# A planned order and engine choice replaced from its 346th operation on

## The chip, the cores and the metric

The kernel runs on one core of a Trainium2 chip. The metric is the device time of one execution in microseconds (us), lower being better. The engines are named as the profile names them: PE (matrix multiply; PEld is its loading of the stationary operand), DVE, ACT and POOL (element-wise work), SP (which issues nearly all DMAs).

## What is computed

Attention with a local window and block summaries, and then two layers that each expand 512 channels to 2048, apply an element-wise function and come back to 512. Cut to what matters:

```
# attention: 2 x 8 heads, 768 positions, 64 channels
k_sum = k.reshape(B, H, 24, 32, D).max(axis=3)
v_sum = v.reshape(B, H, 24, 32, D).mean(axis=3)
scores = concat(local scores within 16 positions, q @ k_sum + log 32)
x = softmax(scores) @ concat(v, v_sum)            # 1536 rows of 512
# first layer
h = x @ w_in                                      # 512 -> 2048
g = (a0 + a1 h + a2 h^2 + a3 h^3) / (1 + |b0 h| + |b1| h^2)
x = g @ w_out                                     # 2048 -> 512
# second layer
h = x @ w_in2
out = (h * cos(h)) @ w_out2
```

## The kernel before

Every matrix product of the two layers is made of three products of a high and a low part (`gh`, `gl` for the activations, two halves of `w` for the weights), which the function `split` makes: one copy to a rounded type (L347 on ACT, L349 on POOL, L352 on DVE) and one subtraction (L806 on POOL or DVE). The weights come from memory as 64-bit numbers into one of three `raw` buffers and are turned to 32 bits by three DVE steps (L789, L793, L797).

The 1536 rows are handled in three blocks of 512. For each block and each slice of 128 of the 2048 inner channels there is a unit: the products into `h` (L946), the element-wise chain (`ew1`, `ew1s` in the first layer: L1233 to L1259; `ew2` in the second: L1314 and L1317 reduce the angle, L1320 is the Sin on ACT, L1323 the product), a `split` into `gh` and `gl`, and four times three matmuls into four accumulators `acc` (L1363, in `mlp_o`). Most units are handled two or four at a time with seven products in place of eight, whose sums share PSUM banks: `mlp_h4` (L1133, 512 columns) and `mlp_h2` (L1182, 256 columns). There a bank that goes on accumulating has first to be read out by a copy (`keep`, on ACT or DVE) or an addition (`plus`, L1146 on DVE), so a later product waits for that read. When PE turns from one block to the next, the four accumulators are spilled to `part` or `room` (L341, L343, L347, L352 by engine) and the sums of the next block are copied back into the same four banks (L347 or L352, out `acc`); the first triple of matmuls into a bank waits for its copy. The attention is interleaved with the first units: transposes of k and q (`ktp`, `qtp`), scores (`sp`, L652), the softmax (L682 on DVE, L686 on ACT, L703 the multiply by the reciprocal sum on POOL or DVE), its transpose (`ptp`, L716) and the product with v (`avp`, L763).

None of this is issued in the order in which the code stands. Each operation is recorded in a `Plan` with the engines that it may run on, and the string `ORDER` gives for each of the 3011 recorded operations which one comes next and which engine takes it:

```
for lo, hi, e in zip(raw[:n], raw[n:2 * n], raw[2 * n:]):
    o = rest.pop(lo + 256 * hi)
    o.eng = "AVPTS"[e]
```

Each engine then executes its own operations in exactly that order. `place` gives every tile the buffer that has been free longest in the same order, so buffers follow from the order too. Nothing in the program holds a time; semaphores between the engines keep the dependences.

Of the kernel before, what the change touches and what calls it, by code (L numbers as in the profile page):

```python
# [35 lines left out]
for _p, _t in (("AA", .143), ("AP", .17), ("AT", .25), ("AV", .14), ("PA", .08), ("PP", .08), ("PT", .15),  # L36
# [25 lines left out]
    "&L_k4w+`9agD1q)+$@PD=GjGSP0hX|m9g7y&DvP;(i8I}gVgE18@+Kj=e}3mQ#Z@O5l$TMBil~HfUv+kx_EHi#q9iXcCt6kf"
    "n75`=|QBa@Au(~dfctQw!d$FXW#+P{J+Wl>X4P-{ik@%82qJI{eIigo0!r|!Kaj_u?XYH`hr?s#_1c&60e02*2i}5IMn0@<b"
    "tq}L}W#-7T#hH<b3LEhGDt<F#H?5qcDLMej%FJ{CVVsq3L<1CI0t2{}Twa+X?vZ>l<KKk2R}aGx!g_&VQW`oIwIz+n)Uh`oF"
    "4=+GW??+^p*;V&Xgx9<vW{dv)EHuYKRYIE(7)=BK~+lU11K?}jMq(x^?6@UFS~e$0c=^V6jB{kp88IL~wcadGDDH(#Cvn;^c"
    "K#NMj$7v408{EaVXtIW?5Kknmw=Up7Uhs*mg4D&ddhtdAj3--acx+of=elq!_@w~wEi^-($KkNT2t8+iia<3?})JsdxGr*~X"
    "*z@xI0^ocYoU~1X*oq<x(obhWavs=`1H=?$QE)qZnPoPKI}tI%V2ruUj#g>PB0>x@C$b={GCx>^0PJ4@&@`L_5O4rm%c<RF2"
    "R3Ye^P5b>NA?j!(J}<!uDfi(A+)q8d_{<?=8FWTQ<-Fthi+Qt4OQZKp|nb>!=a4M&YX~#CV3#+V0|Hob$PKovKGYLnA6>s(9"
    "M3g=ojSGimc{K()L3?tlPdP4QZO=p+5e>w%d!zTe9WFzaPD=VKJ?%Sw56y3(KqXN%qfmUgei`v&q&p%U~ZLA16sZ&*DBy+xa"
    "#n%^SLk!^LtER{3>UWEUZAgQSwhnFNp?r{U)2I`l8V56->m%%AQ$Ag<#P?+4&WKUsJ9-laRCVAs~RG9uITq(H3FsV(Bkjkpt"  # L70
    "D5L}kx;DX~Nr*Lw9bb5Mh!!8c3SHFBkht-2Qh2``ZIx!5B))xEo*6JTbzb{wo$`q?*4jC{wjuX1-e+*%GU(KVizRJVN<g?<u"
# [1533 lines left out]
```

## Time and profile before

| | us |
|---|---|
| median of 3 runs | 590.38 (589.5 to 591.62) |
| the profiled execution | 591.18 |
| its span, first to last instruction | 589.4 |
| PE busy | 573.8 (97% of the span) |
| DVE busy | 529.1 (90%) |
| ACT busy | 451.3 (77%) |
| POOL busy | 355.7 (60%) |

The granted clock of PE is 1.00 over the span. A matmul is on record for longer than the step to the next one, since matmuls overlap, so a PE that is busy on the page may still lose time: how fast it goes is read from the distance of one matmul's start to the next. In the chain of work that ended last, 73% of the span is PE's, and ACT and DVE have 10% each.

### The profile page before, as it was taken

Reading aid. Unit: us, or ns where it says so; the run is one execution under the profiler, and the core shown is the slowest. Engines: PE = TensorE matmul, PEld = TensorE weight load, DVE = VectorE, ACT = ScalarE, POOL = GpSimd, SP = SyncE. Lnnn points to the kernel's source line nnn. Section 1 sums busy time; section 2 is a strip of 40 time slices with the busy share of each in tenths; the row PEclk is TensorE's granted clock in tenths of the full one; section 3 lists DMA queues with packets and bytes.
Section 4 is the critical chain, followed back from the end, with each engine's and each line's share of the span. In section 5 each row is a group of like instructions: output and inputs, shape, how many; then the busy total and the mean of one; then the engine's idle time right before and its main releaser. Section 6 shows DMA issues by size and latency. Waiting matters only on the chain.

```text
span 589.4 us, 10346 instructions
## 1 busy us (share of the span) xinstructions
PE 573.8 (97%) x3564; PEld 476.9 (81%) x3564; DVE 529.1 (90%) x1070; ACT 451.3 (77%) x979; POOL 355.7 (60%) x354
## 2 busy tenths in 40 slices
PE   8879999999999999999999999999999999999997
PEld 7568788888887887888888788888889888888885
DVE  4999999999999999999999999998889897886673
ACT  4989999989889999999899996757447335545343
POOL 4678889765878767777877625347354532554430
PEclk9999999999999999999999999999999999999999
DMA  8988950312122121312103221222231132020004
GB/s 254 245 225 224 252 131 16 112 31 65 51 71 71 41 103 37 108 48 97 53 20 107 73 72 37 71 72 72 72 107 49 62 106 72 1 72 1 1 37 178
DMA packets 68861, 51.83 MB, mean 88 GB/s; under 512 B 37304, under 2 KB 63160, under 8 KB 68808
## 3 DMA queue, kind: packets, MB, share of 16 engines
q1 hardware_dynamic: 68664, 51.03, 29.1%
q8 instruction: 28, 0.46, 0.3%
q14 instruction: 25, 0.20, 0.1%
q10 hardware_dynamic: 144, 0.13, 0.1%
HBM read 47.71 MB, written 3.15 MB: 86 GB/s over the span
## 4 chain that ended last, share of the span: by engine, by line
PE 73%; ACT 10%; DVE 10%; DMA 2%; issue 2%; SPq 1%; POOL 1%; ACTq 0%; DVEq 0%; POOLq 0%
PE acc L1363 34%; PE h L1133 15%; PE h L946 12%; PE h L1182 6%; PE avp L763 2%; ACT sc L686 1%; PE ptp L716 1%; PE sp L652 1%; DVE tt L1246 1%; DVE h L1256 1%; DVE tt L1253 1%; DVE h L1244 1%; DVE tt L1259 1%; DMA raw<-in_moe_w_out_dram 1%; DMA part<-in_k_dram 1%
## 5 line engine op out<-in xcount | busy, mean ns | idle before, releaser
L1363 PE MATMUL acc<-gh,w 128*128 128x512 f32 (+1 forms) x416 | 122.7, 378 | 1.3 <-ACT acc L347 1.3
L1363 PE MATMUL acc<-w,gh 128*128 128x512 f32 x382 | 118.1, 390 | 0.1
L806 POOL TENSOR_TENSOR gl<-tt,gh 128x512 fp32r<-128x512 f32 (+1 forms) x58 | 77.2, 1333 | 58.4 <-DVE gh L352 31.3
L1363 PEld LDWEIGHTS acc<-gh,w 128*128 128x128 f32 x416 | 75.4, 188 | 16.7 <-ACT acc L347 2.4
L1363 PEld LDWEIGHTS acc<-w,gh 128*128 128x128 f32 x382 | 70.5, 188 | 14.2 <-ACT part L341 0.6
L1363 PE MATMUL acc<-gl,w 128*128 128x512 f32 (+1 forms) x208 | 77.6, 373 | 0.0
L1363 PE MATMUL acc<-w,gl 128*128 128x512 f32 x191 | 74.3, 389 | 0.0
L806 POOL TENSOR_TENSOR w<-f,w 128x512 fp32r<-128x512 f32 x47 | 64.4, 1376 | 14.2 <-ACT w L347 13.0
L347 ACT COPY tt<-h 128x512 f32<-128x512 f32 (+1 forms) x68 | 35.2, 528 | 23.6 <-PE h L1133 10.5
L946 PE MATMUL h<-big,w 128*128 128x512 f32 x216 | 52.9, 390 | 0.2 <-DVE tt L1259 0.2
L1320 ACT ACTIVATE h<-h 128x512 f32<-128x512 f32 x48 | 27.3, 582 | 27.2 <-DVE h L1317 27.2
L946 PEld LDWEIGHTS h<-big,w 128*128 128x128 f32 x216 | 40.4, 188 | 9.1 <-DVE tt L1259 0.8
L797 DVE SCALAR_TENSOR_TENSOR f<-raw,f 128x512 int32<-128x512 int32 x64 | 47.4, 743 | 0.3
L1314 ACT ACTIVATE h<-tt 128x512 int32<-128x512 f32 x48 | 28.4, 601 | 24.9 <-DVE tt L1146 7.6
L793 DVE SCALAR_TENSOR_TENSOR f<-raw,f 128x512 int32<-128x512 int32 x64 | 44.7, 701 | 0.2
L1363 PEld LDWEIGHTS acc<-gl,w 128*128 128x128 f32 x208 | 39.1, 188 | 7.1
L1363 PEld LDWEIGHTS acc<-w,gl 128*128 128x128 f32 x191 | 35.8, 188 | 7.5
L1133 PE MATMUL h<-xH,w 128*128 128x512 f32 x120 | 41.5, 389 | 0.0
L347 ACT CAST gh<-tt 128x512 fp32r<-128x512 f32 (+1 forms) x56 | 34.6, 618 | 8.0 <-DVE tt L1323 4.5
L1323 DVE TENSOR_TENSOR tt<-tt,h 128x512 f32<-128x512 f32 x48 | 32.1, 681 | 7.2 <-ACT h L1320 6.9
L1242 POOL TENSOR_TENSOR tt<-tt,tf 128x512 f32<-128x512 f32 x21 | 29.1, 1386 | 14.1 <-ACT tt L1233 13.8
L686 ACT ACTIVATE sc<-sc,mn 128x120 f32<-128x120 f32 x96 | 37.5, 397 | 0.1
(261 smaller groups left out, 1572.1 us busy)
## 6 DMA issues: line engine op xcount, KB each, us to landing
raw<-in_moe_w_in_dram SPq DMA_DIRECT2D x32, 512.0 KB, 3.8
raw<-in_moe_w_out_dram SPq DMA_DIRECT2D x32, 512.0 KB, 3.3
vw<-in_v_dram SPq DMA_DIRECT2D x24, 192.0 KB, 4.1
qk<-in_q_dram SPq DMA_DIRECT2D x10, 256.0 KB, 3.7
out_dram<-part SPq DMA_DIRECT2D x8, 256.0 KB, 2.3
part<-in_k_dram SPq DMA_DIRECT2D x8, 192.0 KB, 3.7
big<-in_v_dram SPq DMA_DIRECT2D x3, 512.0 KB, 8.0
qk<-in_k_dram SPq DMA_DIRECT2D x6, 256.0 KB, 4.5
```

The lines of the kernel that those rows point to most:

```text
L347: nc.scalar.copy(out=o, in_=i)
L686: lambda e, pr=pr, hh=hh, sv=sv: nc.scalar.activation(out=sv()[:, pr, :], in_=sv()[:, pr, :], func=ACTF.Exp, scale=-1.0, bias=mn.t[:, hh, ...
L793: lambda e: nc.vector.scalar_tensor_tensor(out=ft.t.bitcast(I32), in0=lohi()[1], scalar=-0x40000000, in1=ft.t.bitcast(I32), op0=ALU.bitwis ...
L797: lambda e: nc.vector.scalar_tensor_tensor(out=ft.t.bitcast(I32), in0=lohi()[0], scalar=29, in1=ft.t.bitcast(I32), op0=ALU.logical_shift_r ...
L806: lambda e: E[e].tensor_tensor(out=lo(), in0=x(), in1=hi().bitcast(F32), op=ALU.subtract),
L946: nc.tensor.matmul(out=h.t[:, 0:n], lhsT=lt, rhs=rt[:, kk, cs], start=(k0 == 0 and i == 0), stop=(k0 == 2 and i == 5))
L1133: nc.tensor.matmul(out=bank.t, lhsT=lt, rhs=rt, start=start and i == 0, stop=stop and i == 5, skip_group_check=True)
L1182: nc.tensor.matmul(out=bank.t[:, c], lhsT=lt, rhs=rt, start=start and i == 0, stop=stop and i == 5, skip_group_check=True)
L1242: lambda e: E[e].tensor_tensor(out=U(), in0=U(), in1=Z(), op=ALU.add))
L1314: lambda e: nc.scalar.activation(out=H().bitcast(I32), in_=S_(), func=ACTF.Identity, scale=1.0 / PER, bias=0.25))
L1323: lambda e: E[e].tensor_tensor(out=S_(), in0=S_(), in1=H(), op=ALU.mult))
L1363: nc.tensor.matmul(out=dst, lhsT=lt, rhs=rt, start=(un.start and not have and i == 0), stop=(un.stop and i == 2), skip_group_check=have)
```

## The change

The string `ORDER` is another one. Nothing else in the program differs: the same 3011 operations with the same operands, of which 971 run on DVE in place of 974, 876 on ACT in place of 877, 327 on POOL in place of 323, and 696 on PE and 141 on SP as before. The order and the engines were searched anew, on a replay that was given the landing times of the DMAs as a trace showed them and the load of ACT's function table. The first 345 operations are the same, which in the trace of before reach to about 51 us on each engine.

```diff
 ORDER = (
-    "c-rk)$&Mt+aW&s!-}faWBDcz=GHc1&y0-3SZ!^Qeh>M0C5`>81ff(^XP#|?7bf6$m2VF=VBuJky2LbvFopcd&67(~4H;*E}K"
...
+    "c-rk*NslE-QZ`>A!eig#MZ}AUx9>}?l}oK%dv*6P>QT)wNQkOFphnX)!w7^pa6rQ#1V}9oAS8al`~WUo;K;AyfV+8Q&4~*qg"
...
 )
```

Three places in the order are shown here. The first is ACT at the turn from the first layer to the second, where the table for Sin is loaded; `acc_4262`, `acc_4267` and `acc_4266`, `acc_4289` are accumulators into which the next block's sums are copied back, the other `acc` are the finished ones that are spilled. Before:

```order
L341 ACTIVATE part<-acc_4116 128x512
L1251 ACTIVATE h<-tf 128x512
L341 ACTIVATE part<-acc_4172 128x512
L347 COPY acc_4262<-part 128x512
L347 COPY acc_4267<-part 128x512
L1320 ACT_TABLE_LOAD
L1320 ACTIVATE h<-h 128x512
L341 ACTIVATE part<-acc_4140 128x512
L341 ACTIVATE part<-acc_4089 128x512
L347 CAST gh<-tt 128x512
L347 COPY acc_4308<-part 128x512
```

The same place in ACT's order after the change:

```order
L1251 ACTIVATE h<-tf 128x512
L341 ACTIVATE part<-acc_4069 128x512
L347 COPY acc_4266<-part 128x512
L1320 ACT_TABLE_LOAD
L1320 ACTIVATE h<-h 128x512
L341 ACTIVATE part<-acc_4189 128x512
L341 ACTIVATE part<-acc_4145 128x512
L347 COPY acc_4289<-part 128x512
L347 CAST gh<-tt 128x512
L341 ACTIVATE part<-acc_4139 128x512
L347 COPY acc_4301<-part 128x512
```

One accumulator in place of two is spilled and refilled ahead of the load, and the third copy into an accumulator no longer stands behind a `gh` cast; PE's two small groups (L1182) stand behind one triple into a refilled accumulator, where they stood behind two.

The second place is PE within one `mlp_h4` of the first layer, at 185.8 us of the trace of before; `xL,pt`, `qT,pt` and so on are the operands of its products. Before:

```order
L1133 MATMUL h<-xL_111,pt 128x512
L1133 MATMUL h<-xH_110,qk 128x512
L1133 MATMUL h<-qT_2030,pt 128x512
L1133 MATMUL h<-qT_2032,pt 128x512
L1133 MATMUL h<-qT_2030,qk 128x512
L1133 MATMUL h<-sc,pt 128x512
L1133 MATMUL h<-pt 128x512
L1133 MATMUL h<-sc,qk 128x512
L1363 MATMUL acc_2748<-gh,w_2236 128x512 x2
L1363 MATMUL acc_2748<-gl,w_2236 128x512
L1363 MATMUL acc_2775<-gh,w_2236 128x512 x2
L1363 MATMUL acc_2775<-gl,w_2236 128x512
```

The same products in PE's order after the change:

```order
L1133 MATMUL h<-xL_111,pt 128x512
L1133 MATMUL h<-xH_110,qk 128x512
L1363 MATMUL acc_2684<-gh,w_2228 128x512 x2
L1363 MATMUL acc_2684<-gl,w_2228 128x512
L1363 MATMUL acc_2684<-gh,w_2359 128x512 x2
L1363 MATMUL acc_2684<-gl,w_2359 128x512
L1133 MATMUL h<-qT_2018,pt 128x512
L1133 MATMUL h<-qT_2043,pt 128x512
L1133 MATMUL h<-qT_2018,qk 128x512
L1133 MATMUL h<-sc,pt 128x512
L1133 MATMUL h<-pt 128x512
L1133 MATMUL h<-sc,qk 128x512
```

Two triples into an accumulator now stand between two products that stood back to back, and three triples follow ahead of the next product (`qk,w`) where two did.

The third place is DVE in the stage of the attention, some 200 rows into its list. Before, around a reciprocal (L699) of the softmax:

```order
L352 COPY room<-big 128x8x96
L806 TENSOR_TENSOR gl<-tt,gh 128x256
L699 RECIPROCAL su<-su 128x8
L352 CAST xH_110<-avp 128x4x128
L774 TENSOR_TENSOR xL_111<-avp,xH_110 128x4x128
L797 SCALAR_TENSOR_TENSOR f<-raw,f 128x512
```

And in the changed order:

```order
L789 TENSOR_SCALAR f<-raw 128x512
L774 TENSOR_TENSOR xL_111<-avp,xH_110 128x4x128
L699 RECIPROCAL su<-su 128x8
L703 TENSOR_TENSOR sc<-sc,su 128x480 x2
L793 SCALAR_TENSOR_TENSOR f<-raw,f 128x512 x2
L797 SCALAR_TENSOR_TENSOR f<-raw,f 128x512 x2
```

Four of the softmax multiplies (L703) that POOL did are DVE's now, two of them here.

## Rows read from the trace of the kernel before

**Rows 1.** The page's first part: busy us, share of span, instructions by engine.

```profile
PE 573.8 (97%) x3564; PEld 476.9 (81%) x3564; DVE 529.1 (90%) x1070; ACT 451.3 (77%) x979; POOL 355.7 (60%) x354
```

**Rows 2.** Busy time by stretch: us, PE, PEld, DVE, ACT, POOL, clock, DMA share, GB/s.

```profile
51.00:130.00 79.00, 78.73 (x831) 65.84 (x832) 76.50 (x236) 73.37 (x220) 63.37 (x62) 1.00 0.45 116
130.00:345.00 215.00, 213.07 (x935) 173.71 (x934) 211.34 (x349) 203.32 (x361) 155.88 (x131) 1.00 0.22 72
345.00:575.00 230.00, 230.00 (x1147) 195.70 (x1147) 196.31 (x330) 128.57 (x244) 103.59 (x102) 1.00 0.17 53
```

**Rows 3.** Waits of PEld, 130 to 590 us: total us, times, longest.

```profile
PEld acc L1363 <- ACT acc L347: 2.4, 3, 1.5
PEld h L1133 <- ACT tt L347: 0.9, 2, 0.7
PEld h L946 <- DVE tt L1259: 0.8, 2, 0.6
PEld h L1133 <- DVE tt L1146: 0.7, 2, 0.4
PEld acc L1363 <- ACT part L341: 0.6, 1, 0.6
```

**Rows 4.** Timeline at the table load: start, us, engine, what [idle before <-releaser].

```profile
334.02 0.69 DVE L1317 SCALAR_TENSOR_TENSOR h<-h,tt 128x512 f32<-128x512 int32 x1
...
334.68 1.28 ACT L1320 ACT_TABLE_LOAD   x1
...
335.97 0.58 ACT L1320 ACTIVATE h<-h 128x512 f32<-128x512 f32 x1
...
336.46 1.08 ACT L341 ACTIVATE part<-acc 128x512 f32<-128x512 f32 x2
...
337.42 0.63 ACT L347 CAST gh<-tt 128x512 fp32r<-128x512 f32 x1
...
337.93 0.61 ACT L347 COPY acc<-part 128x512 f32<-128x512 f32 x1
...
338.59 0.73 PE L1363 MATMUL acc<-gh,w 128*128 128x512 f32 x2 [1.31 <-ACT acc L347]
```

**Rows 5.** PE's timeline inside one `mlp_h4` of the first layer.

```profile
182.93 1.52 PE L1133 MATMUL h<-vw,sc 128*128 128x512 f32 x6
...
184.70 0.50 PE L1133 MATMUL h<-xH,pt 128*128 128x512 f32 x1 [0.24 <-ACT tt L347]
...
186.22 0.73 PE L1133 MATMUL h<-qT,pt 128*128 128x512 f32 x2
...
187.71 0.61 PE L1363 MATMUL acc<-gh,w 128*128 128x512 f32 x2
...
188.39 0.61 PE L1363 MATMUL acc<-gh,w 128*128 128x512 f32 x2
...
189.25 0.50 PE L1133 MATMUL h<-qk,w 128*128 128x512 f32 x1
```

**Rows 6.** The chain of waits in order of time: pieces that ran without a stop.

```profile
273.65 1.36 PE h L1133 x6
...
348.86 1.43 PE h L1182 x12
```

**Rows 7.** Waits of PEld in the stage of the attention, 51 to 130 us.

```profile
PEld sp L652 <- POOL raw L565: 1.0, 1, 1.0
...
PEld avp L763 <- ACT pt L347: 0.8, 2, 0.5
PEld ptp L716 <- issue: 0.8, 3, 0.4
```

**Rows 8.** DVE's timeline, steps that follow each other, 188 to 191 us.

```profile
188.51 0.68 DVE L1146 TENSOR_TENSOR tt<-h,tt 128x512 f32<-128x512 f32 x1
189.11 0.67 DVE L1253 SCALAR_TENSOR_TENSOR tt<-tt,h 128x512 f32<-128x512 f32 x1
```

**Rows 9.** DMA issues by line: KB each, median us from issue to landing.

```profile
qk<-in_k_dram SPq DMA_DIRECT2D x6, 256.0 KB, 4.5
```

More of the change, by code (lines that the diff above doesn't have):

```diff
@@ L62 @@
[L62 to L71, printed above, removed]
@@ L102 @@
[L102 to L104 removed]
+    "c-rk*NslE-QZ`>A!eig#MZ}AUx9>}?l}oK%dv*6P>QT)wNQkOFphnX)!w7^pa6rQ#1V}9oAS8al`~WUo;K;AyfV+8Q&4~*qg"
+    "wm@jGoMGex!Gr*edeC^>tExTPN&_Z>xybsRf#CyPhwwqo*(~15PUCe#|ecG;9B&Tw(*y_e}wZ(<FX~)%CI}K{W)LpDJ+YT3*"
+    "E@<?BUQEn{5mLCUf0m#eX|bNSJ&cC%+=GfL8z`!ds_t|D<rZZ6zc#<-3=LU}rnQHasxc22L&Z<MtnIS`<-4E%?H+ATlkJMJc"
@@ new lines @@
+    "t*z_)Xt*C~*v2Jj2uH|(2ld>5_`XJ_m<gm>HBy57{!>&Jm@-)><rE{dWniW6ei`z*_b>!E#JUqSY#iI_}o&Wj}euIv6bzDzI"
+    "A(u48!VUw(v+bD`&KP%vUXa-4e1AqM>x{1%ujZ-r)K7I@aj<ZQ!SUO?;J`b}Hk_3kP;j5Q#V)4&H?40HD<E~ivxg*?ZGIL$a"
+    "{(d?>1VU`PxwU<=-ncLsxtT*ohN$-6p8f2P#m=x`U4~{l2REL$yEt~E$Ow$8@(2DKs4fehxjfm)t({u~R(?n<%X#EjjJ0ihy"
+    "|(z!w1cVR?Cat~VY9z#8gpjZiBk_Km^I|4>%L=L_`i5VJ^BYgJTDB>H00hXajn|f1{>S9^WVx{J58C%zB5f)JFh*?1u;11>2"
+    "8-s>}nI9E)I+3$$l9!px;j3zGdUrAK8j_ls124#aV1c)=&P)wOua;8w{D<#@I0WD@xCH8}qCGERM#btNE19-~GqGZ(c3g?B7"
@@ new lines @@
+    "!J+4dw!_ppkGbrZ)hfUn_r_2_mS1nET?1dpD?)h@`QfM=_-kH4Q~!SmctswY(#M$y8b`@GDOG_O1vQc>hGteN*Pd1A&N{4f0"
+    "7uI^^@`FvEj`>>9-|2lMCzxMqiPsjeV=9xQ)-6A@7e>V)>FdBv3iR<sjZtMDfF!Uw(ZsX0Kw`rE9UsgXz)4V9WyzmOoi`|3U"
+    "Mo}2Z7~MQC;;su*->HNo&s=8Fy0k%rTVfxNb!B^=F(aHLNy@lYnL)q}?=#OZ7To3}@_mar%yHhnrGyY8g*?x<i+Gkv+k}N<L"
+    "jK08z#9A#z~Jd3n*YUlcQj+p!C;_<RjdJ)xxr?$WC}53oH6PqZVAPB;M}sC7QEVv<1<-Z)HI)Z^eQ52!{!f`VsS=hGut{cbL"
+    "5iEVK-g2bl%7$PbOqK9T75WDpC%ss_M$7G01$ilYH8&mL<$bS#i^}SC_>_(GCkJtMYa?%J+jc@pd_hb~_10BD0isT||=Y<ar"
@@ new lines @@
+    "#A7D*V^?Kr#|<pn)2iU)O81Owvdk8(dF?CPiFa_Y~h=S|1piQ&5WAnb)Lyla@)xs{40IXnB&&`yLcilb${s4Rfk9;dd^-5R$"
+    ";AGpuY3+H_2`j8xUj(r3%-E0E!G+2p8i^a3s#Z5PvjfCXpe0bUp$B%#K1fX7Tx!IVDGhVE}S;919X$Hw0>UcW2CJ>cjKKv?_"
+    "`51gL*m<wkkq5+yb0>rD;p<x#1aNU7=%e6~=>a&0OZRgjE<Qiw*80uM<*S3mO_Lk57ca)Qx8B@(*o`iD%YS;sFWV#3!_$3Tv"
+    "&!6T>es8)(yZVQtIbqmGroXPcP#SX8|Sd!WYvbHgLF~N7wKS{7HONaCQGFLtX41`(C~UX9cO?3_gxs4aU54rZpxqxA@}|0;$"
+    "j?*zl`e$-cl$Q;Mp$tJ{7(QzP^5&Q@aAkPDvt?$wPjd5YxDJ-x>A!xuouBY?Oo&QJFs^<OiH*neR)@qafL8<*5ON2)R$G>r_"
@@ L105 @@
+    "M0wn2oQ_I*JIi+fX@G_9j(6<Y~tLs-#RWmukA-Bg!-50%;k^-p(Xs-RE~BlaqzyjKwXrX8X>kX}g@F|}ESjRey{k%c|{J<V_"
+    "_!!qXh1H~z#)tmGkhGJu*eH&M)VOo}Y)nmOQ$WQf)R?@?SVfFgbb3lu?)(f3)EaJX!&?cpQdqM&*T_38y>0^_MTfePTLiZz$"
+    "nch{UMoT2UYi8t5wRFU!e^*fl4++{7vV&7ZU&n?=1g5J*C#-MWs6e`~xvpg03W=^^6mQ++kZuI}zq%Gx7se$htP(HHMyAheS"
+    "}w3wXm5djqBVv=v0Nw`;oA8-Ina}Y-qjoHPY1f~5KT8N80a4+fWfCGtYrsD)eD|ZbuU4>uTgS0-}^%Fw5`kjlZ+y%80hmR#m"
+    "5AzfOGt>bnUS^&oNXFt~iS)a^U|B4tyOq"
 )
```

62 lines of the change are left out of this document (25 added, 37 removed).

## The prediction

> **What bounds the kernel now.** I read the page's busy times first, then the busy times by stretch, then PE's waits in each stretch, and the timelines where those waits lie. PE is busy for 97% of the span and DVE for 90% [rows 1]. That does not yet say that PE is full, since matmuls overlap on record. The starts say it: a group of six matmuls of 512 columns that meets no wait takes 1.36 us, 0.227 a matmul, and a triple 0.68 [rows 6]. The work of PE is the same before and after, so all that an order can give back is time in which PE steps slower than that. By stretch [rows 2]: from 345 to 575 us PE is busy without a break, 230.0 of 230.0 us; next to nothing is to be had there. From 130 to 345 DVE is busy for 211.3 of 215 us and ACT for 203.3, and PE's weight loads wait there, by the five largest rows, 5.4 us in all: 3.0 for accumulators that are being spilled and refilled, 0.9 and 0.7 for banks of an `mlp_h4` that are being read out, 0.8 for DVE's L1259 [rows 3]. A weight load runs ahead of its matmul, so these are upper bounds of what PE lost. From 51 to 130, the attention, waits are many and small [rows 7]; several are on "issue", which means on nothing that an order moves. Before 51 us nothing changes. The end is the same in both orders: a last triple, one copy on ACT and DVE each, and their stores.
>
> **The change part by part.** *The table load.* This is the largest single stop. Behind two copies into accumulators ACT loads the table for 1.28 us, does the Sin, two spills (1.08), a cast (0.63) and only then the copy that PE needs; PE starts at 338.59 after 1.31 us without a matmul [rows 4]. Together with the other two waits on copies and the one on a spill the weight loads wait 3.0 us around it [rows 3]; PE's share I put at 2.3 (1.5 for the long one, which is also its weight load's longest wait, and about half of the other 1.5). Now the new order, by the same durations, from the start of the triple into `acc_4266`: PE has that triple, 0.68, and the two small groups, 1.43 [rows 6], so it wants `acc_4289` after 2.11 us. The accumulator `acc_4069` was finished four triples earlier, 2.7 us, so ACT can spill and refill it (0.54 and 0.56) by -1.4 and load the table by -0.1; Sin lasts to 0.45, two spills to 1.5 and the copy to 2.1. That meets PE within 0.1 us. The next refill comes after a cast, a spill and a copy, 0.63 + 0.54 + 0.56, at 3.8; PE wants it after three more triples, at 4.15. I take 0.3 as what is left of 2.3: a gain of 2.0. If ACT comes to the load late, PE waits for all of that lateness, since nothing covers it; the Sin's operand is DVE's L1317 at 334.02, which ended only just ahead of the load [rows 4]. Bounds: a gain of 2.3, and none.
>
> *The chain of products at 183 to 191 us.* In the trace the group at 182.93 takes 1.77 us to the next start in place of 1.36, the one at 184.70 1.52, the one at 186.22 1.49, and the triple at 188.39 0.86 in place of 0.68 [rows 5]: 0.41 + 0.16 + 0.13 + 0.18 = 0.9 us lost. The new order puts two triples between the second and third of these groups and one more ahead of the last, 2.0 us in which DVE and ACT may read the banks. The first two groups stay back to back. I take a gain of 0.6 (bounds 0.9 and a loss as below).
>
> *Other stalls of that kind.* Of the 5.4 us there remain about 1.3 at other places, near 212 and 230 us. The rows of order there show a product moved by one triple to either side and no clear widening; I take 0.3, between 0 and 1.3. Against it stands a place near 314 us: the last three products of a `mlp_h4` now stand back to back, where two triples divided them. The like place of before is the one just costed, where a back-to-back group lost 0.16 to 0.41 [rows 5]; I take a loss of 0.4 (bounds 0 and 0.9, that whole place again).
>
> *The attention stage.* The number of turns between transposes, scores, and matmuls of the layers is nearly the same in both orders (55 for 56), so the "issue" share stays. Four softmax multiplies move from POOL to DVE, which shortens the path to their transposes, but puts them on the fuller engine (76.5 of 79 us, POOL 63.4 [rows 2]). The transposes of k come closer together: a `qk` buffer is refilled between a transpose and one that now follows after some 4.3 us of PE's own work, where it was 5 or more, and the load takes 4.5 us [rows 9], so a stop of up to half a us can arise. Against a possible gain of the 1.0 and 0.8 on the longest waits [rows 7] I take 0 here, with bounds of a gain of 1.5 and a loss of 1.5.
>
> *The engines' totals* (971 DVE operations for 974) cost or give nothing themselves: past 345 us ACT and POOL are idle for nearly half the time or more [rows 2], so the four operations more on POOL hide there.
>
> Sum: -2.0 - 0.6 - 0.3 + 0.4 + 0 = -2.5 us. Against the profiled execution, 591.18 (a span of 589.4 and 1.8 around it), that is 588.7. The median of the runs is 590.38, 0.8 below the profiled one, so the forecast is 587.9.
>
> **A rule weighed.** The trace's load of the table lasts 1.28 us, and the Sin starts at 335.97, where the load ends [rows 4]. The Trainium skill, ScalarE: Activation LUTs, section What ACT_TABLE_LOAD costs, gives 1283 ns for the load, as here, and about 1380 ns more of a drain, 2.66 us for a change of set. The trace shows no such drain between the load and the Sin. By that rule the copy into `acc_4289` would come 1.4 us later than worked out above and the gain would be 1.1 instead of 2.5, an estimate of 589.3; its chance, 2 in 100, is counted in the rival "same".
>
> **The rivals.** *All stalls go.* The table's 2.3, the 0.9 at 183 us, the 1.3 elsewhere: -4.5 us, 585.9. For it: nothing but order causes them, and DVE has 3 steps less in all. Against it: the margins above are 0.1 to 0.4 us, and two places are tighter than before.
>
> *The stops move.* ACT or DVE reach the table load or the read of a bank half a us later than I add up, and half of the gain goes into new stops of 0.2 to 0.5 us: -0.8 to -1.6, about 589.3. For it: DVE is 98% busy [rows 2], so delays there are not made up. Its size follows from the margins.
>
> *DVE becomes the bound, and it is slower.* Up to the addition at 188.51 that ends a bank's read [rows 8], DVE has three operations more in the new order (20 come in, 17 go, the four multiplies among those that come). At the pace of 0.60 us from one step's start to the next [rows 8] three steps are 1.8 us. A second such addition, 18 us later, has five more ahead of it, 3.0 us. In the trace PE started the product behind the first 0.06 us after the addition was through, so 1.8 us there is a stop of 1.8 unless DVE's own gaps, 1 to 3% of the stretch, close by as much. If none closes, PE is 3.0 later by 210 us, every later block is late with it because DVE stays full to 345, and the gain at the table is lost because L1317 comes late: +3.0 and no gain, 593.4. It decides from the point where DVE's extra work exceeds what its gaps can absorb, about 2.5 us from 51 to 130 [rows 2]. Against it: the gaps exist, and fewer bubbles are what an order can bring.
>
> *The change doesn't do what it says* cannot be here, since the order of every engine is read off the program.
>
> **How the numbers follow.** Forecast, -1.8 to -3.5: 0.37. All stalls go, -3.5 to -5: 0.18. The stops move, -1.8 to +1.8: 0.31. DVE the bound, +1.8 and above: 0.14. A difference of 0.3%, 1.8 us, is about what a measurement of this kernel can tell from none. So faster by more than that has 0.55, within it 0.31, slower 0.14. The range reaches from 585.5, which leaves the last part of "all stalls go", to 592.0, which leaves most of "DVE the bound".
>
> **What would show it.** Right: in the new profile PE's wait on a copied accumulator next to the table load is under 0.4 us, the third product of the `mlp_h4` near 185 us follows its triples at the 0.23 us step, and from 345 us on PE runs without a break as before, some 2.5 us earlier. Wrong: a PE wait of over 1 us on ACT there, or several waits on DVE's L1146 or a `gl` between 150 and 330 us, which would be the slower rival; or new waits on `qk` or `pt` before 130 us that cost over 1.5.

## The result and the profile after

The changed kernel takes 595.06 us, the median of six runs (593.77 to 595.58), and the kernel before 590.26 in the same comparison. The ratio is 1.0071, with a 95% interval of 1.0051 to 1.0091. The change makes the kernel 0.7% slower. The forecast was 587.9, in a range of 585.5 to 592.0: wrong in sign, and the time lies outside the range.

The profiled run of after took 595.58, with a span of 593.9 us. Its busy times, in the columns of [rows 1]:

```profile
PE 575.0 (97%) x3564; PEld 478.0 (80%) x3564; DVE 534.9 (90%) x1067; ACT 452.9 (76%) x978; POOL 368.3 (62%) x358
```

DVE does three operations less than in [rows 1] and is busy 5.8 us longer. That is the first thing to see: not the number of its steps grew, but the length of some. (These counts give only the difference: 227 operations run on another engine than before.)

Where PE lost time is told by its busy time in three stretches (columns as in [rows 2]). First before, cut anew:

```profile
51.00:145.00 94.00, 93.73 (x897) 78.27 (x898) 91.33 (x260) 87.56 (x245) 72.51 (x69) 1.00 0.40 104
145.00:203.00 58.00, 57.74 (x252) 46.73 (x251) 57.08 (x93) 52.48 (x92) 46.58 (x42) 1.00 0.19 63
203.00:345.00 142.00, 140.33 (x618) 114.54 (x618) 139.43 (x233) 136.65 (x244) 100.16 (x83) 1.00 0.25 79
```

and after:

```profile
51.00:145.00 94.00, 91.69 (x914) 76.41 (x907) 92.19 (x259) 85.63 (x242) 70.55 (x69) 1.00 0.41 106
145.00:203.00 58.00, 56.35 (x244) 44.98 (x243) 57.51 (x92) 50.60 (x88) 46.82 (x40) 1.00 0.21 64
203.00:345.00 142.00, 140.69 (x622) 114.99 (x621) 140.33 (x233) 134.92 (x238) 103.36 (x86) 1.00 0.23 71
```

PE stood idle 0.3, 0.3 and 1.7 us before, and 2.3, 1.7 and 1.3 after. The loss lies in the attention (+2.0) and from 145 to 203 us (+1.4); behind 203 us there is a small gain, 0.4, and from 345 to 575 PE is busy for 230.0 of 230.0 us, as in [rows 2]. The weight loads' waits in 130 to 345 us, which answer to [rows 3], have new names:

```profile
PEld h L1133 <- ACT tt L347: 1.6, 2, 1.3
PEld acc L1363 <- POOL gl L806: 1.6, 2, 1.0
PEld acc L1363 <- ACT acc L347: 1.0, 2, 0.8
PEld h L1133 <- DVE tt L1146: 0.8, 1, 0.8
PEld h L1133 <- DVE tt L1300: 0.7, 1, 0.7
```

The wait on copied accumulators fell from 2.4 to 1.0, in the direction that was forecast. Waits on `gl` of POOL, on DVE's L1300 and one of 1.3 us on a `tt` of ACT are new. To see why, take DVE, POOL and PE at 158 to 165 us, timelines with start and length:

```profile
158.75 1.05 DVE L789 TENSOR_SCALAR f<-raw 128x512 int32<-128x512 int32 x1
159.72 0.73 DVE L1300 SCALAR_TENSOR_TENSOR tt<-tt,co,h 128x512 f32<-128x512 f32 x1
...
160.98 0.68 DVE L793 SCALAR_TENSOR_TENSOR f<-raw,f 128x512 int32<-128x512 int32 x1
161.58 1.52 DVE L789 TENSOR_SCALAR f<-raw 128x512 int32<-128x512 int32 x1
163.02 0.68 DVE L1297 SCALAR_TENSOR_TENSOR h<-tt,h 128x512 f32<-128x512 f32 x1
```

```profile
158.22 1.29 POOL L806 TENSOR_TENSOR qk<-f,pt 128x512 fp32r<-128x512 f32 x1
161.24 1.57 POOL L806 TENSOR_TENSOR gl<-tt,gh 128x512 fp32r<-128x512 f32 x1 [1.73 <-ACT gh L347]
```

```profile
160.51 0.50 PE L1133 MATMUL h<-xH,big 128*128 128x512 f32 x1 [0.33 <-DVE tt L1300]
...
164.43 0.50 PE L1133 MATMUL h<-xH,big 128*128 128x512 f32 x1 [0.88 <-ACT tt L347]
```

An L789 takes 0.42 us elsewhere. These two began while a step of POOL was running (158.22 to 159.51, and 161.24 to 162.81) and ended 0.29 us behind POOL's end: 1.05 and 1.52 us. The next reading of a bank (L1300, L1297) came late by as much, 0.63 and 1.10 us, and PE stopped at both places, the second time on a copy of ACT (`tt`) that had itself waited for the L1297. L1300 and L1297, one input of which is a PSUM bank, take their usual length beside a running POOL. Before had the same two L789 in another place, in one row at 156.65, between two steps of POOL:

```profile
156.65 0.76 DVE L789 TENSOR_SCALAR f<-raw 128x512 int32<-128x512 int32 x2
```

I call a DVE step **held** if it lasts over 0.1 us longer than its form does undisturbed. In the whole trace of before 35 steps are held, by 13.9 us in sum; in that of after 54, by 26.3. Every one of them overlaps a step of POOL. They end 0.27 to 0.29 us behind POOL's end where they have one input (L789), and 0.51 to 0.56 behind it where they have two inputs from SBUF (L793, L797, L806, L1080), two ends aside. From 51 to 345 us, where PE can be made to wait, the sums are 4.9 and 9.9 us. (By what is taken as undisturbed, such sums move by up to 0.6.)

### The profile page after: what moved, and what is told of

Read it like the earlier page. It is cut to its first block, busy times and chain, and to the rows that moved or that the text cites. A ratio compares the mean times of both kernels' runs of the same rounds, so it can differ in the third digit from the quotient of the medians.

```text
span 593.9 us, 10356 instructions
## 1 busy us (share of the span) xinstructions
PE 575.0 (97%) x3564; PEld 478.0 (80%) x3564; DVE 534.9 (90%) x1067; ACT 452.9 (76%) x978; POOL 368.3 (62%) x358
## 4 chain that ended last, share of the span: by engine, by line
PE 69%; DVE 20%; ACT 5%; issue 3%; DMA 2%; SPq 1%; DVEq 0%; ACTq 0%
PE acc L1363 35%; PE h L1133 18%; PE h L946 8%; PE h L1182 6%; ACT sc L686 1%; DVE h L1297 1%; DVE tt L1284 1%; DVE tt L1294 1%; DVE f L793 1%; DVE tt L1286 1%; DVE tt L1300 1%; DVE tt L1080 1%; DMA part<-in_k_dram 1%; DVE tt L1253 1%; DVE tt L1246 1%
## 5 line engine op out<-in xcount | busy, mean ns | idle before, releaser
L806 POOL TENSOR_TENSOR gl<-tt,gh 128x512 fp32r<-128x512 f32 (+1 forms) x67 | 89.1, 1330 | 57.7 <-ACT gh L347 24.3
L806 POOL TENSOR_TENSOR w<-f,w 128x512 fp32r<-128x512 f32 x47 | 65.0, 1385 | 18.0 <-ACT w L347 17.0
L347 ACT COPY tt<-h 128x512 f32<-128x512 f32 (+1 forms) x70 | 37.2, 538 | 20.9 <-PE h L1133 10.6
L793 DVE SCALAR_TENSOR_TENSOR f<-raw,f 128x512 int32<-128x512 int32 x64 | 49.7, 780 | 0.3
L797 DVE SCALAR_TENSOR_TENSOR f<-raw,f 128x512 int32<-128x512 int32 x64 | 48.0, 752 | 0.5
L347 ACT COPY part<-acc 128x512 f32<-128x512 f32 x55 | 31.8, 588 | 16.2 <-PE acc L1363 16.0
L1317 DVE SCALAR_TENSOR_TENSOR h<-h,tt 128x512 f32<-128x512 int32 x48 | 32.8, 693 | 12.3 <-ACT h L1314 11.6
L347 ACT CAST gh<-tt 128x512 fp32r<-128x512 f32 (+1 forms) x54 | 32.8, 608 | 10.8 <-DVE tt L1323 7.2
```

Source lines behind the costliest of these rows:

```text
L347: nc.scalar.copy(out=o, in_=i)
L793: lambda e: nc.vector.scalar_tensor_tensor(out=ft.t.bitcast(I32), in0=lohi()[1], scalar=-0x40000000, in1=ft.t.bitcast(I32), op0=ALU.bitwis ...
L797: lambda e: nc.vector.scalar_tensor_tensor(out=ft.t.bitcast(I32), in0=lohi()[0], scalar=29, in1=ft.t.bitcast(I32), op0=ALU.logical_shift_r ...
L806: lambda e: E[e].tensor_tensor(out=lo(), in0=x(), in1=hi().bitcast(F32), op=ALU.subtract),
L1317: lambda e: nc.vector.scalar_tensor_tensor(out=H(), in0=H().bitcast(I32), scalar=-PER, in1=S_(), op0=ALU.mult, op1=ALU.add))
```

## The experiments

Three theories stood against each other. **A**: steps held by POOL stop PE. **B**: the rival of the prediction, more DVE work ahead of the additions that free banks. **C**: the landings of the first loads differ between runs, and the order is not the cause.

For each kernel the table gives its median, the ratio to before in the same comparison with its interval, the held time from 51 to 345 us, and PE's lost time by section. Lost time is, for each group of PE, the time to the next group's start less what it takes without a wait [rows 6], added over the groups of a section in the profiled run (attn_loads_two and after_pool_halves are told of below). The sections end at the 345th operation (51 us), the 948th (145), the 1247th (203) and the 2032nd (354).

```
kernel                 median  ratio [95%]              held   to 51  to 145  to 203  to 354
before                 590.26                            4.9    14.9     6.3     1.2     3.6
after                  595.06  1.0071 [1.0051, 1.0091]   9.9    15.8     8.4     3.2     2.9
after_again            593.95  1.0069 [1.0044, 1.0094]   8.6    14.0     7.4     3.2     2.9
attn_new               593.08  1.0045 [1.0029, 1.0061]   6.3    14.1     8.3     1.2     4.2
mid_new                592.68  1.0031 [1.0018, 1.0044]   7.4    13.8     6.2     3.7     3.3
late_new               590.03  0.9989 [0.9978, 1.0001]   6.3    14.1     6.2     1.2     3.3
after_multiplies_back  596.58  1.0097 [1.0077, 1.0117]  12.4    14.0    10.9     3.3     2.9
after_six_moved        593.28  1.0050 [1.0032, 1.0067]   6.7    14.9     8.6     2.3     3.0
after_eight_moved      593.10  1.0039 [1.0024, 1.0055]   6.7    13.3     8.1     2.3     3.0
after_nine_moved       593.73  1.0062 [1.0039, 1.0084]   5.4    17.1     9.7     1.9     2.7
late_new_moved         590.38  0.9998 [0.9982, 1.0014]   6.4    13.9     6.2     1.2     3.4
mid_new_again          592.57  1.0042 [1.0027, 1.0057]   7.3    13.7     6.2     3.7     3.2
mid_new_moved          591.74  1.0021 [1.0009, 1.0033]   5.1    15.0     6.2     2.5     3.3
attn_new_moved         594.56  1.0067 [1.0051, 1.0082]   4.9    13.7     9.9     1.2     4.2
attn_loads             596.13  1.0113 [1.0097, 1.0128]   5.1    13.9    10.8     1.5     4.2
parts_joined           591.95  1.0021 [1.0007, 1.0035]   7.3    14.3     6.2     4.2     3.0
```

**Which section costs what.** Three kernels take one section each from the changed order.

```diff
-all 3011 operations in the order and on the engines of before
+attn_new: operations 346 to 948 as in the change
+mid_new: operations 949 to 1247 as in the change
+late_new: operations 1248 to 3011 as in the change
```

> The order and engines of the changed kernel up to its 948th operation (about 145 us), then those of before to the end. Theory A (steps on DVE that start while POOL is in a step are held until POOL's step ends; the changed order brings more of these meetings, and PE stops behind them): the stops that PE's trace of the changed kernel shows up to 145 us and that before's does not add up to 2.2 us, so this kernel is 2.2 us slower than before, 592.5, with the stops at 66 and 117 us in its profile. Theory B (the rival of the prediction: more DVE work ahead of the additions that free banks, put there by the four softmax multiplies that came from POOL): all of the loss is laid down here, since the multiplies lie here: 4 us or more slower, 594.5. Theory C (the landings of the first loads differ from run to run and shift everything; the order is not the cause): within 1 us of before.

> The order of before, but from the 948th to the 1247th operation (about 145 to 203 us) that of the changed kernel. Theory A: the stops at 159, 163, 173 and 193 us come, less the stops of before at 183 to 188 that go: 2.0 us slower, 592.3; the DVE steps held by POOL between 150 and 203 us add up to about 3.5 us where before has 1.2. Theory B: no more than 0.5 us slower, as no multiply moves between engines here and the additions come with the same work ahead of them. Theory C: within 1 us of before.

> The order of before up to the 1247th operation (about 201 us), then that of the changed kernel to the end. Theory A, by the stops counted in the two traces: 0.7 us faster than before, 589.6; the stop behind the load of ScalarE's table shrinks from 1.5 to about 0.7, and stops on POOL's gl of 0.9 and 0.5 us take its place. The prediction's own sum for this part (table load -2.0, the place near 314 us +0.4, other stalls -0.3) would give 1.9 us faster, 588.5. Theories B and C: as the prediction's sum, or as before.

Measured against the 590.48 of their comparison: +2.6, +2.2 and -0.45 us; the last is not told apart from no change. Together +4.35, which is nearly all of the change's +4.8. So the loss belongs to the order and lies in the first two sections, as theory A said of each within 0.4 us; theory B expected 4 and 0.5, theory C 1 at most, and both fall. A's figures were added up from the stops in the trace of after, whatever made them: this comparison tells where the loss is, and not yet that held steps make it. In late_new PE's wait on the copy behind the table load is 0.5 us, and two waits on POOL's `gl`, 0.8 together, took the place of what was gained.

**The mechanism by itself.** A small program has the kernel's three kinds of DVE step and POOL's two.

```
shift  (as L789)  DVE tensor_scalar, one input from SBUF            its line 42
merge  (as L793)  DVE scalar_tensor_tensor, two inputs from SBUF    its line 46
bank   (as L1146) DVE tensor_tensor, inputs from PSUM and SBUF      its line 51
POOL: subtraction of two tensors, line 59; copy of one, line 62
```

> A small program of its own, which writes zeros: it computes nothing of the reference. Three kinds of DVE step on 128x512, as the kernel has them: the shift of L789 (one input from SBUF, short form), the merge of L793 (two inputs from SBUF), an addition with one input from PSUM as L1146. Each runs alone, then beside POOL's subtraction of two 128x512 tensors in a row, then beside POOL's copy with one input; at last the merge beside POOL's subtraction of 256. Theory A: alone 0.42, 0.60 and 0.60 us from start to start; beside POOL's subtraction the shift and the merge run once for each of POOL's steps, 1.3 to 1.9 us, ending 0.28 and 0.55 us behind POOL's end, and the addition from PSUM keeps 0.60; with the halves the merge takes about 0.75 to 1.3. Theories B and C: every kind keeps its duration within 10%, since what the large kernel shows comes from its waits.

The kinds ran mixed and not one after the other, so they are read by place. From 12 to 27 us, merges and shifts in turn beside POOL's subtractions (groups: count, busy us and mean ns):

```profile
L46 DVE SCALAR_TENSOR_TENSOR g<-raw,a 128x512 int32<-128x512 int32 x6 | 9.4, 1567 | 0.0
L42 DVE TENSOR_SCALAR f<-raw 128x512 int32<-128x512 int32 x6 | 8.9, 1480 | 0.0
```

From 76 to 91 us each of them stands between additions that read a bank, beside POOL's copies:

```profile
L51 DVE TENSOR_TENSOR o<-hp,b 128x512 f32<-128x512 f32 x12 | 8.1, 678 | 0.0
L42 DVE TENSOR_SCALAR f<-raw 128x512 int32<-128x512 int32 x10 | 4.1, 410 | 0.0
L46 DVE SCALAR_TENSOR_TENSOR g<-raw,a 128x512 int32<-128x512 int32 x3 | 2.0, 676 | 0.0
...
L62 POOL TENSOR_SCALAR p<-p 128x512 f32<-128x512 f32 x17 | 14.4, 845 | 1.3
```

In the first place a DVE step waits for POOL's to end; the shift takes 1.48 in place of 0.41. In the second DVE keeps its lengths and POOL is the one that waits: its copy, 0.62 us where DVE is idle, takes 0.845 in the mean of this stretch. The addition that reads a bank takes 0.68 at every place. In the whole kernel no step goes another way: in the trace of after 82 of DVE's L789, L793, L797, L806 and L1080 began inside a step of POOL, and all ended behind it; 173 of its 512-column steps that read a bank (nine lines, L1146 to L1300) began there too, and none of them took over 0.75 us. So the two engines exclude each other for such steps, and the one that began first goes through. Theory A's durations came true, with the addition that POOL can be held too. That the smaller subtraction would shorten the hold was not shown: beside POOL's steps of 256 columns DVE won nearly every meeting.

The Trainium skill has this: SBUF — State Buffer, section Who interferes with whom, says of the ports that VectorE and GpSimd share that "Issue order, not op shape, decides who blocks". The trace agrees, and the change's own program shows how finely. It was run again:

> The changed kernel once more, on the chip of the next three, as their measure. Its trace of before's result shows 3.7 us more stops of PE behind 51 us than the trace of before, and 0.8 more ahead of 51, where the two programs are the same. If the landings of the first loads made part of the loss (theory C), this run stands 0.8 us or more below 595.1; by theories A and B it is 594 to 595.5 again, 3.7 to 4.8 slower than before.

It took 593.95, 1.1 less than at first, with a spread of 592.6 to 596.4, so theory C is good for about that much and not for the sign. What its profile shows at 113 us is worth more than its time. DVE, POOL and PE in the first profile of after:

```profile
115.36 1.79 DVE L1080 TENSOR_TENSOR tt<-xH,xL 128x512 f32<-128x512 f32 x1
...
115.33 1.28 POOL L806 TENSOR_TENSOR qT<-tt,qT 128x512 fp32r<-128x512 f32 x1
...
118.41 1.89 PE L946 MATMUL h<-big,w 128*128 128x512 f32 x7 [0.56 <-DVE big L774]
```

and in the second of the same program:

```profile
113.35 0.68 DVE L1080 TENSOR_TENSOR tt<-xH,xL 128x512 f32<-128x512 f32 x1
...
113.34 1.85 POOL L806 TENSOR_TENSOR qT<-tt,qT 128x512 fp32r<-128x512 f32 x1
...
115.47 2.88 PE L946 MATMUL h<-big,w 128*128 128x512 f32 x12
```

The two steps start within 0.03 us of each other. In the first run POOL is 0.03 us ahead on record, DVE waits 1.1 us and PE stops; in the second the starts are 0.01 apart, POOL's the earlier on record (too little to tell which was first), DVE goes through, POOL waits 0.57, and there is no stop. The same order gives both. PE's lost time in the attention is 1.0 us less in the second run (7.4 for 8.4).

**Theory B undone.** The four multiplies go back to POOL.

```diff
 four L703 of the attention (sc<-sc,su 128x480)
-on DVE
+on POOL
```

> The changed kernel with the four softmax multiplies (L703) that it moved from POOL to DVE on POOL again, at the places where they stand; nothing else differs. Theory B: the extra work ahead of the additions goes, 2.4 us of DVE, so 1.5 to 3 us faster than the changed kernel, 592 to 593.5. Theory A: DVE loses four steps of 0.6 (one of them held for 1.05 at 67 us) but POOL, which takes 1.0 for each, holds others in their place: within 1 us of the changed kernel, 594 to 596.

It became slower still, 596.6. Theory B expected a gain of 1.5 to 3 us and falls; theory A's "within 1 us" missed as well. That the multiplies on DVE were a help is likely and not shown, as the two intervals overlap. The first multiply now stands ahead of POOL's L565 (65.25 and 66.19 us), and PE waits for that:

```profile
67.51 1.04 PE L568 MATMUL vmp<-raw,vsel 128*24 128x512 f32 x2 [1.63 <-POOL raw L565]
```

**Moving the held steps, whole kernel.** Six, then eight, then nine steps of the changed order are moved by a few places (of the six, five change place in DVE's own list). The core of it, as DVE's order:

```diff
 L1297 SCALAR_TENSOR_TENSOR h<-tt,h 128x512
-L789 TENSOR_SCALAR f<-raw 128x512
 L1300 SCALAR_TENSOR_TENSOR tt<-tt,co,h 128x512
 L1294 SCALAR_TENSOR_TENSOR tt<-tt,h 128x512
+L789 TENSOR_SCALAR f<-raw 128x512
 L793 SCALAR_TENSOR_TENSOR f<-raw,f 128x512
 L789 TENSOR_SCALAR f<-raw 128x512
 L1297 SCALAR_TENSOR_TENSOR h<-tt,h 128x512
```

> The changed kernel with six DVE steps moved by one to three places, so that they no longer begin while POOL is in a step (by the times of its trace): an L1080 near 72 us and one near 115, two L789 near 159 and 162, an L793 near 166 and one near 328. Every step keeps its engine, and no work is added or left out. Theory A (DVE steps held by POOL): the stops of PE behind these six go, 0.3 + 0.86 + 0.48 + 1.05 + 0.4 + 0.87 = 4.0 us by the trace of the changed kernel; some meetings will come up elsewhere, so 2.0 to 4.0 us faster than the changed kernel, 591.0 to 593.0, and the sum of the time by which DVE steps of 51 to 345 us are held falls from 10 to about 5 us. Theory B (more DVE work ahead of the additions): the work ahead of them is the same but for these six, so within 0.5 us of the changed kernel, 595. Theory C (landings): the same as B.

> As the kernel with six DVE steps moved, and two steps of POOL exchanged with a neighbour: the w of L806 near 61 us now stands ahead of the L565 that waits for a load, and the gl of L806 near 339 us ahead of a step for a weight (with its L349). The trace of the changed kernel shows PE stopped 1.0 us on that w and 0.5 us on that gl; neither of these stops comes from a held DVE step. If POOL's own order makes them, this is 1.0 to 1.5 us faster than the kernel with six moved, 590 to 592; if the w waits for its input and not for POOL's turn, it is the same.

> The kernel with six DVE steps moved, whose trace shows three more steps held by POOL, each ahead of a stop: an L797 near 60 us (0.7 us), an L797 near 166 (1.0) and an L793 near 328 (1.1, the one that took the place of the step moved there). These three are moved behind two to seven of DVE's next steps; nothing else differs. Theory A: PE's stops at 167, 171 and 172 us (1.1 us together) and the 1.0 at 333 us go, of which a wait on a copied accumulator at 338 may take 0.4 back: 1.2 to 2.0 us faster than with six moved, 591.3 to 592.1. If what is left of the loss has other causes than held steps, it is the same as with six moved, 593.

Six moves gave 593.28: 0.7 us below the changed kernel's second measurement and 1.8 below its first, where 2 to 4 were expected. The stops at 117 and 159 us went and the one at 163 fell from 1.05 to 0.19, but stops of 0.4 each at 74 and 78, 0.61 at 137 and 0.27 at 168 came, and the one at 335 stayed: the L793 that I moved there let the next L793 be held in its place (1.1 us). The two exchanges on POOL gave nothing more (expected 1.0 to 1.5). Three further moves took the held time down to 5.4 us and gave nothing either; the section to 203 us improved to 1.9, and the attention lost 1.1 more, behind an L565; 1.2 to 2.0 us had been expected. With runs that spread by 3 us this comparison decides little, so I went to one section.

**Moving the held steps, one section.** mid_new has the order of before up to 145 us and runs that agree closely. Beside what is shown here, one further L797 moves on by four places.

```diff
 L1294 SCALAR_TENSOR_TENSOR tt<-tt,h 128x512
+L789 TENSOR_SCALAR f<-raw 128x512
 L793 SCALAR_TENSOR_TENSOR f<-raw,f 128x512
...
 L1286 SCALAR_TENSOR_TENSOR tt<-tt,co,h 128x512
 L797 SCALAR_TENSOR_TENSOR f<-raw,f 128x512
-L793 SCALAR_TENSOR_TENSOR f<-raw,f 128x512
 L1146 TENSOR_TENSOR tt<-h,tt 128x512
 L1294 SCALAR_TENSOR_TENSOR tt<-tt,h 128x512
+L793 SCALAR_TENSOR_TENSOR f<-raw,f 128x512
```

> The kernel mid_new once more, as the measure on the chip of the next two: 592.7 and 2.2 us slower than before, by all theories.

> The kernel mid_new with five DVE steps moved in its new section, and nothing else: the two L789 that POOL holds at 155 and 158 us (0.65 and 1.10 us), the L793 held at 162 (1.10), and an L797 that would take the place of that one, stand behind two to seven steps that read a bank. Theory A: PE's stops at 155 and 159 us (0.59 + 1.06) go, and perhaps the 0.4 at 170: 1.2 to 2.0 us faster than mid_new, 590.7 to 591.5, within 0.2% of before. If held steps only come along with a loss that has another cause, it is the same as mid_new, 592.7.

The moves brought 592.57 to 591.74, 0.8 us, where 1.2 to 2.0 were expected, and the ratio from 1.0042 to 1.0021, 1.2 us. The intervals still overlap a little, but 8 of the 12 runs lie below the lowest of all 19 of mid_new's order (592.09). PE at the two stops, first mid_new_again:

```profile
156.73 0.50 PE L1133 MATMUL h<-xH,big 128*128 128x512 f32 x1 [0.42 <-DVE tt L1300]
...
160.64 0.50 PE L1133 MATMUL h<-xH,big 128*128 128x512 f32 x1 [0.89 <-ACT tt L347]
```

then mid_new_moved, PE and the two L789 on DVE:

```profile
157.31 0.39 PE L1133 MATMUL h<-xH,big 128*128 128x512 f32 x1
...
160.36 0.50 PE L1133 MATMUL h<-xH,big 128*128 128x512 f32 x1 [0.16 <-ACT tt L347]
```

```profile
157.54 0.42 DVE L789 TENSOR_SCALAR f<-raw 128x512 int32<-128x512 int32 x1
...
158.60 0.42 DVE L789 TENSOR_SCALAR f<-raw 128x512 int32<-128x512 int32 x1
```

No work was changed, only meetings were avoided: the steps have their 0.42 again, one stop is gone and the other falls from 0.89 to 0.16. PE's lost time in the section falls from 3.7 to 2.5, of 1.2 in before. So held steps cause about half of this section's loss; with the moves the held time is down to 5.1 us, about that of before. The other half is made by a stop behind an L1146 at 189 us (0.6; in after at 193), two of 0.4 at 170 us behind a `gh` of POOL and a `gl` of DVE, and one of 0.3 at 145, less the 1.0 that before loses at 183 to 188.

**The attention.** Moves there did not separate the causes.

```diff
+attn_new_moved: two L1080 and an L797 of DVE later, the w of L806 ahead of an L565 on POOL
+attn_loads: two loads raw<-in_v earlier in SP's queue
+attn_loads_two: attn_loads, and the two L1080 later
```

> The kernel attn_new (593.1, 2.6 us slower than before) with four moves: the two L1080 of DVE that POOL holds near 70 and 115 us, an L797 held near 60, and POOL's w of L806 ahead of the L565 that waits for a load. Theory A with POOL's own order as the second cause: the stops at 115 us (0.88), 70 (0.55) and 58 to 60 (1.04) go, some 0.9 of new stops at 74 and 78 us may come as in the kernel with six moves: 0.8 to 2.0 us faster than attn_new, 591.1 to 592.3. If the attention's loss lies in something else, it stays at 593.

> The kernel attn_new (593.1, 2.6 us slower than before) with two loads of raw<-in_v issued earlier in SP's queue: one ahead of the qk<-in_k and the vw<-in_v that stood before it, as in the order of before, one ahead of one qk<-in_q. In the trace of attn_new POOL stands idle for 2.4 us on these landings, with the w of L806 queued behind it; before has no such wait. If the queue's order is the attention's second cause, POOL's wait falls below 1 us and PE's stops at 58 to 60 and 65 us (0.5 to 0.6 each, 1.6 together) shrink: 0.8 to 1.6 us faster than attn_new, 591.5 to 592.3. If the landings come no sooner, or the stops are made by held DVE steps (theory A alone), it stays within 0.5 us of attn_new.

> As attn_loads, and the two L1080 of DVE that POOL holds near 70 and 115 us are moved behind the next two steps, as in the kernel with six moves. Theory A: the stops at 70 (0.55) and 115 us (0.88) go; 0.5 to 1.4 us faster than attn_loads, 590.4 to 591.5. If those stops have another cause, as attn_loads.

All three became slower than attn_new, at 594.56, 596.13 and 597.31, and every expectation missed. In attn_new_moved the L797 that I moved is held in its new place as well (1.49 us, to 62.24), and what needs it comes late: POOL's next copy, and the second load `raw<-in_v`, issued at 62.27 where attn_new has 60.75, with an L565 behind its landing. The weight loads wait 1.6 us for that L565 and 1.3 for the copy. In attn_loads a load put ahead makes the `q` behind it late (issued at 60.76 for 57.55). PE's wait there, from 45 to 76 us:

```profile
PE qtp L607 <- DMA qk<-in_q_dram: 3.6, 1, 3.6
```

Behind that stop, which ends at 65.29, the clock falls (columns as in [rows 2]):

```profile
62.00:64.00 2.00, 0.00 (x0) 0.00 (x0) 1.93 (x6) 1.34 (x5) 0.68 (x2) 1.00 0.94 264
68.00:70.00 2.00, 2.00 (x33) 1.51 (x32) 0.00 (x0) 0.70 (x2) 2.00 (x4) 0.50 0.24 39
```

The granted clock is 0.50, the 1.2 GHz level, from 66.7 to 70.1 us; in the profiled run of attn_new it stays at 1.00 there. All nine runs of the two kernels with moved loads have a mean clock of 0.994 to 0.997, six of attn_new's seven one of 0.999 or 1.00. By my estimate, half the speed for 3.4 us costs up to 1.7 us, so part of what these two lost is the clock's.

The attention's 2.6 us are thus the order's (attn_new shows that). By starts, the stops that attn_new has there and before hasn't are 1.5 us behind the two held L1080 (71 and 116 us) and 1.6 behind landings and POOL's row (59, 60 and 66 us). How much of the time the holds make and how much the loads and the L565 stays open: the one pair of kernels that differs by the two L1080 alone, attn_loads and attn_loads_two, had only 0.2 us held in them to begin with.

**Three that were meant to gain.** In the first, POOL's subtractions of 512 columns in L806 are issued as two of 256.

```diff
-             lambda e: E[e].tensor_tensor(out=lo(), in0=x(), in1=hi().bitcast(F32), op=ALU.subtract),
+             lambda e: halves(e, n, lo(), x(), hi().bitcast(F32)),
...
+        m = o.shape[1] // 2
+        for h in (slice(0, m), slice(m, 2 * m)):
+            E[e].tensor_tensor(out=o[:, h], in0=a[:, h], in1=b[:, h], op=ALU.subtract)
```

> The changed kernel with each subtraction of 512 columns that POOL does in split (L806) issued as two of 256; order and engines stay. POOL's work grows by about 0.2 us for each of some 75 in 51 to 345 us. Theory A: a DVE step waits for a shorter POOL step, so the sum held in 51 to 345 us falls from 9.9 to 5 to 7 us, and PE's stops behind held steps with it: 1 to 2.5 us faster than the changed kernel if POOL's longer row is not waited for; if PE waits for gl and w instead, up to 1 us slower, with waits on L806 of POOL in the place of waits on DVE. Theory B: no shorter stops on DVE, 0 to 2 us slower.

> The order of before up to the 1247th operation, then that of the changed kernel (the kernel late_new), with two exchanges near 328 and 339 us: the L793 that POOL holds stands behind two steps that read a bank, and gl ahead of POOL's step for a weight. Theory A: the stops of 0.6 and 0.2 on gl go, 0.5 to 1.0 us faster than late_new and 1 to 1.5 faster than before, 589. Theory B: as late_new.

> The order of before up to its 1137th operation (about 178 us), then the changed one with two DVE steps (the L793 that POOL holds near 322 and 324 us) moved behind steps that read banks. Theory A: none of the losses up to 178 us; the stops of before at 183 to 189 us (1.05) become 0.7 at 193; the stop of 1.0 on gl goes, and a wait of 0.4 more on a copied accumulator comes: 0.3 to 1.5 us faster than before, 589 to 590. Theory B: as the kernel late_new, 590.

None of the gains that theory A expected came. Halves made it slower, 599.78 us, ratio 1.0162 [1.0138, 1.0186]. From 51 to 345 us there are more meetings, 35 held steps for 20, and their sum grows from 9.9 to about 13 us, so that theory A's forecast of a smaller sum fails. POOL's row is longer too. PE stands idle for 0.9 us from 145 to 203 (1.7 in after), but for 4.0 from 203 to 354 (1.3 in after), on `gl`, on DVE's steps and on copied accumulators in turn. late_new_moved is no faster than late_new: as above the next L793 took the hold, and what the second `gl` gave (0.5) went into the stop on the copied accumulator, 1.16 where it was 0.70. parts_joined is slower than before: at its joint PE waits 2.5 us for a `gl` of POOL and for a copied accumulator, which are done within 0.02 us of each other; neither order has that wait there, and behind it the granted clock is 0.50 from 180.9 to 184.3. No version beats the kernel before by more than can be measured; late_new is the nearest.

## Why the prediction was wrong

By sections the forecast was 0 for the attention, -0.6 to 203 us and -1.9 behind (table load, other stalls, the place near 314 us). The kernels with one new section each measured +2.6, +2.2 and -0.45.

*What bounds the kernel* held: PE from 345 us on has no break in either kernel, and all that moved lies ahead.

*The table load, -2.0.* Its own wait did shrink, from the 1.31 of [rows 4] to 0.55, more than the 0.4 that was to show the forecast right, and a wait for POOL's `gl` came in the place of the gain. PE and ACT in after:

```profile
336.33 0.50 PE L1363 MATMUL acc<-gl,w 128*128 128x512 f32 x1 [0.60 <-POOL gl L806]
...
342.75 0.73 PE L1363 MATMUL acc<-gh,w 128*128 128x512 f32 x2 [0.55 <-ACT acc L347]
```

```profile
339.34 1.28 ACT L1320 ACT_TABLE_LOAD   x1
340.63 0.58 ACT L1320 ACTIVATE h<-h 128x512 f32<-128x512 f32 x1
...
342.08 0.62 ACT L347 COPY acc<-part 128x512 f32<-128x512 f32 x1
```

PE's lost time from 330 to 350 us is the same in both kernels, 2.3 us. The step that failed is the sum that followed ACT alone from the start of one triple, with PE taken as waiting for nothing else: the `gl` of a triple just ahead came from POOL late, 334.66 to 336.27, and DVE and ACT had been late with its `gh`. The load lasts 1.28 us and the Sin begins at its end, here too; the drain that was weighed is seen in neither trace.

*The chain of products, -0.6.* Half right. The product behind the two triples follows them at the 0.23 step, as the forecast said, and the six of 182.93 in [rows 5] took 1.77 to the next start, and in after the like group takes 1.36. But the next product behind it stops on just the addition that the slower rival had named [rows 8]:

```profile
186.30 1.52 PE L1133 MATMUL h<-vw,sc 128*128 128x512 f32 x6
187.66 0.39 PE L1133 MATMUL h<-xH,pt 128*128 128x512 f32 x1
...
194.33 0.50 PE L1133 MATMUL h<-qk,w 128*128 128x512 f32 x1 [0.39 <-DVE tt L1146]
```

By starts that is 0.7 us lost, against about 1.0 gained: a net 0.3 for the 0.6.

*Other stalls, -0.3, and the place near 314 us, +0.4.* The stalls at 211 and 230 us are gone, some 1.0 gained, more than was taken and within the bounds; the tightened place cost about 0.2.

*The attention, 0 with bounds of 1.5.* It cost 2.6 alone (attn_new), outside the bounds. I had looked at turns, at the multiplies and at one load of k. What stops PE there are two held L1080, POOL's L565 behind a landing, and the w queued behind that. Of these only the L565 stood among my rows ([rows 7], 1.0), and I took it for a possible gain.

*145 to 180 us* was no term at all, and the section to 203 us cost 2.2. This is the step that failed most. I let every DVE step take its usual 0.60 from start to start [rows 8], whatever POOL did meanwhile, and compared only counts. In its place the runs showed steps that wait for POOL's: 9.9 us held for 4.9 from 51 to 345 us, and in mid_new, where PE loses 2.5 us more than before, 1.2 of them gone when such steps were moved. What makes the other 1.3 is told by its stops alone. Rows that told otherwise could be had from the trace of before, L793's on its page: an L789 takes 0.42 undisturbed and an L793 0.68, and their groups have means of 454 and 701 ns.

```profile
L793 DVE SCALAR_TENSOR_TENSOR f<-raw,f 128x512 int32<-128x512 int32 x64 | 44.7, 701 | 0.2
...
L789 DVE TENSOR_SCALAR f<-raw 128x512 int32<-128x512 int32 x64 | 28.7, 454 | 2.1 <-POOL w L806 1.2 <-DMA raw<-in_moe_w_out_dram 0.8
```

```profile
L793 DVE SCALAR_TENSOR_TENSOR f<-raw,f 128x512 int32<-128x512 int32 x64 | 49.7, 780 | 0.3
...
L789 DVE TENSOR_SCALAR f<-raw 128x512 int32<-128x512 int32 x64 | 33.3, 526 | 1.4 <-DMA raw<-in_moe_w_out_dram 1.3
```

The first fence is before, the second after: 64 steps each, 5.0 us more for L793 and 4.6 for L789.

*The rivals.* "DVE becomes the bound" had the right sign, the right engine and, by luck, nearly the right time, 593.4; it also named L1146 and `gl`. Its price came from the wrong cause, the number of operations ahead of an addition, and the multiplies put back, which gained nothing, speak against it. "The stops move" described the table load.

Three things stay open: the attention's causes, as said, and two more. The medians differ by 3.7 to 4.8 us, and the profiled runs by 3.5 (after) and 2.5 (after_again) behind 51 us; the rest is not in a profile that I have. And the prefix that both share lost 13 to 17 us of PE in different runs; in the profiled run of after 0.9 us of the difference lies there, where the granted clock was 0.50, the 1.2 GHz level, from 32.7 to 36.1 us, after PE had been busy for 1.15 of the 2 us from 30 on.

```profile
30.00:32.00 2.00, 1.15 (x32) 1.01 (x32) 1.96 (x7) 1.74 (x8) 0.93 (x2) 1.00 0.98 293
32.00:34.00 2.00, 1.34 (x7) 1.37 (x8) 1.78 (x13) 2.00 (x10) 1.77 (x2) 0.68 1.16 285
34.00:36.00 2.00, 2.00 (x11) 2.00 (x11) 1.39 (x5) 0.32 (x2) 0.15 (x1) 0.50 0.99 298
```

The clock does not make the loss: two of after's six runs have a mean granted clock of 0.996, and five of the 22 runs of before that stand beside attn_new have 0.994 to 0.997; the others, at 0.999 and above, have medians of 594.6 and 590.4.
